# Windowed head-wise convolution and ELU feed-forward: the first super tile's TensorE order from a model, a part of a weight copy on ScalarE, new last turns, one load moved

## The chip, the core and the metric

The kernel runs on one core of a Trainium2 chip. Five engines work from queues of their own and meet only at semaphores: TensorE (PE, with its weight load as PEld), VectorE (DVE), ScalarE (ACT), GpSimd (POOL) and SyncE (SP, which here only issues transfers). The metric is device time in microseconds for one execution; lower is better.

## What is computed

`x` is 8 x 4096 x 192, in 8 heads of 24 channels. Each head has 7 weights over the current and the 6 preceding positions, normalised by a softmax. The result is 32768 tokens of 192 values, and goes through a feed-forward layer of width 2048 with ELU:

```python
w = softmax(weight)                                   # (8 heads, 7 taps)
att[b, s, h] = sum over k of w[h, k] * x_pad[b, s + k, h]
h = att @ w_in                                        # 192 -> 2048
g = np.where(h > 0.0, h, np.exp(np.minimum(h, 0.0)) - 1.0)
out = g @ w_out                                       # 2048 -> 192
```

## The kernel before

**Tiling.** A super tile is 1024 tokens; there are 32 (`NS`). Tokens are split in two groups g of 512. The 2048 hidden features are 16 slices q of 128 (`NQ`). A pair step n = 16 s + q (512 in all, `NP`) makes slice q of super tile s for both groups: units (n, 1) and (n, 0).

**What PE does.** The array is used as two row groups rt of 64 rows, which work side by side. Three kinds of items fill it:

- h (line 835): three matmuls of 512 columns for one unit, rt = group. They need the attention result `att` and `w_in`, which stands twice, in partitions 0 to 63 and again in 64 to 127 (the upper half, for row group 1).
- c (line 808): the convolution of a later super tile as matmuls with a band matrix; four items m to a super tile, each with two matmuls in row group 0 and then two in row group 1, into one bank.
- o (line 858): output matmuls of 192 columns. For a half k = 2 s + half (256 tokens) and a group g they add all 16 slices into one accumulator bank. Both row groups write that bank, in turns that are handed over by the semaphore `s_turn`; a turn is a range of slices in one row group.

**One unit's way.** PE makes H in a PSUM bank, ACT writes E = exp(H) (line 608), POOL clamps E to at most 1 (line 565), DVE writes gT = max(H, E - 1) (line 698). H's bank is free only after DVE. PSUM has 8 banks (`NBANK`), shared by units, convs and accumulators.

**What sets the order.** Before anything is emitted, a planner in Python walks through all pair steps with one clock for each row group. Each item has a fixed cost (line 44: 216 ns for h, 82.5 for o, 102.5 for c), a bank is chosen as the one freed first by fixed holding times (line 48), and the items are sorted by their planned clocks into `pe_order`. ACT's, DVE's and SP's orders follow from the same plan. PE executes `pe_order` strictly; `wait_bank` (line 711) waits for whatever held the bank before.

The lines around the change:

- For n < 24 (`UNTIL`) the clocks are held to at least 1160 ns a pair step (`PACE0`); before the steps n = 1, 2 and 3 `warm` plans one matmul on zeros (line 733).
- Convs of super tile 1 are planned at n = 7, 8, 9, 10 (`EARLY_CONV`). The first accumulators start at n = 4 for group 0 and n = 8 for group 1 (`EARLY_O`), one slice a step; from half 1 on a turn has two slices (`QB`).
- The tail (lines 215 to 236): after the last h, row group 0 does its turns of group 0's open halves and then those of group 1, row group 1 the other way round.
- `w_in` comes in three column parts (`WCOLS`). Parts 0 and 1 are copied to the upper half by DVE (line 623), part 2 (slices 8 to 15) by one SP transfer (line 897); an h item of row group 1 with q of 8 or more waits for it on `s_wd` (line 829).
- POOL issues the loads of x (line 483) between its clamps, at the units listed in `x_before` (lines 265 to 274). The second load of the last super tile is cut in two, since its last window ends at the end of x; both parts are issued at the same unit (lines 487 to 489).

```python
    for n in range(NP):
        if 0 < n < EARLY_O[0]:
            warm(WARM[1])
        if n < UNTIL:
            clock[:] = [max(c, PACE0 * n) for c in clock]
```

Of the kernel before, what the change touches and what calls it, by code (L numbers as in the profile page):

```python
# [49 lines left out]
EARLY_CONV = (7, 8, 9, 10)  # L50
EARLY_O = (4, 8)
PACE0, UNTIL = 1160.0, 24
X_AT = ((2, 1, 1), (1, 1, 0))
ZERO_AT = 8


def bass_lightweight_conv__then__act_elu_kernel(
# [36 lines left out]
    def take_bank(what):  # L94
        if what not in bank_of:
            b = min(range(NBANK), key=lambda b: freed[b])
            assert freed[b] < float("inf")
            bank_of[what], prior[what] = b, occupant[b]
            occupant[b], freed[b] = what, float("inf")

    def h_items(n, r):
        def issue(j):
            take_bank(("h", n, r))
            plan.append((clock[r], ("h", n, r, j)))
            freed[bank_of["h", n, r]] = clock[r] + MM_H + HELD["h"] if j == 2 else float("inf")

        return [(MM_H, lambda j=j: issue(j), None) for j in range(3)]

    def c_items(m, rt):
        def issue(q):  # L110
            take_bank(("c", m))
            plan.append((clock[rt], ("c", m, rt, q)))
            if q == HU - 1:
                conv_half[m] = rt + 1
                if rt == 1:
                    freed[bank_of["c", m]] = clock[1] + MM_C + HELD["c"]

        gate = (lambda: conv_half.get(m) == 1) if rt else None
        return [(MM_C, lambda q=q: issue(q), gate) for q in range(HU)]

    def o_items(k, g, rt, qs, visit, first, final):


        todo = [(q, kb) for q in qs for kb in range(2)]

        def issue(i):
            q, kb = todo[i]
            take_bank(("a", k, g))
            starts, ends = first and i == 0, final and i == len(todo) - 1
            item = ("o", k, g, rt, q, kb, visit if starts else None, ends)  # L130
            plan.append((clock[rt] - AHEAD, item))
            if ends:
                visits[k, g] = visit + 1

        gate = lambda: visits.get((k, g), 0) == visit
        return [(MM_O, lambda i=i: issue(i), gate) for i in range(len(todo))]
# [21 lines left out]
    def warm(count):  # L158
        what = ("w", len(plan) + 1)
        take_bank(what)  # L160
        freed[bank_of[what]] = max(clock)
        plan.append((max(clock) - AHEAD, what + (count,)))
        clock[:] = [max(clock)] * 2

    def evacuated(items, k, g):
        took, issue, gate = items[-1]

        def last():
            issue()
            freed[bank_of["a", k, g]] = max(clock) + MM_O + HELD["a"]  # L170

        items[-1] = (took, last, gate)
        return items
# [11 lines left out]

    conv_steps = {}
# [13 lines left out]
    for n in range(NP):  # L200
        if 0 < n < EARLY_O[0]:
            warm(WARM[1])
        if n < UNTIL:
            clock[:] = [max(c, PACE0 * n) for c in clock]
        lists = [[], []]
        convs = conv_steps.get(n, [])
        for m in convs:
            lists[0] += c_items(m, 0)
        lists[0] += block_items(n, 0, 0) + block_items(n, 1, 0) + h_items(n, 0)
        lists[1] += h_items(n, 1)  # L210
        for m in convs:
            lists[1] += c_items(m, 1)
        lists[1] += block_items(n, 0, 1) + block_items(n, 1, 1)
        emit(lists)
    tail = [[], []]
    for second in range(2):
        for rt in range(2):
# [3 lines left out]
            if second == 0:  # L221
                for kk, q0, q1, v, first in (
                    (k, QB * b, late, 2 * b, True),
                    (k + 1, 0, late, 0, True),
                    (k, late, NQ, 2 * b, False),
                    (k + 1, late, NQ, 0, False),
                ):
                    if kk < NK and q0 < q1:
                        tail[rt] += o_items(kk, g, rt, range(q0, q1), v, first, not first)
            else:  # L230
                for kk, q0, v in ((k, QB * b, 2 * b), (k + 1, 0, 0)):
                    if kk < NK:
                        tail[rt] += evacuated(
                            o_items(kk, g, rt, range(q0, NQ), v + 1, True, True), kk, g
                        )
# [28 lines left out]

    x_before = {}
    for s in range(2, NS):
        for u, ahead, gr in X_AT:
            before = 0
            for item in act_order:
                before += item[0] == "h"  # L270
                if item == ("c", CU * s + u):
                    break
            if s + ahead < NS:
                x_before.setdefault(before, []).append((s + ahead, gr))
# [6 lines left out]
    with ExitStack() as stack:  # L281
# [69 lines left out]
        s_wd = sema("s_wd")  # L351
        s_band = sema("s_band")
# [115 lines left out]
        def _gpsimd(g: bass.BassGpSimd):  # L468
            W = Waits(g)

            def load_x(s, gr):
# [15 lines left out]
                if s == NS - 1 and gr == 1:  # L487
                    windows(0, NWIN - 1, P)
                    windows(NWIN - 1, NWIN, GS - CW * (NWIN - 1) + PAD)
# [85 lines left out]
        def _scalar(a):  # L575
# [24 lines left out]
            for item in act_order:  # L600
# [4 lines left out]
                elif item[0] == "h":  # L605
# [4 lines left out]
                    ).then_inc(s_exp)  # L610
                else:
# [96 lines left out]
        def _tensor(pe):  # L708
# [16 lines left out]
            for item in pe_order:  # L725
# [94 lines left out]
                elif item[0] == "h":  # L820
                    _, n, r, j = item
                    s, q = divmod(n, NQ)
                    if j == 0:
                        part = next(k for k in range(3) if FC * q < WCOLS[k][1])
                        W(s_w[part], 48)
                        if r == 1 and part < 2:
                            W(s_wc, part + 1)
                        elif r == 1:
# [44 lines left out]
        def _sync(sy):  # L873
# [22 lines left out]
            c0, c1 = WCOLS[2]  # L896
# [42 lines left out]
```

## Time and profile before

| what | value |
|---|---|
| median of four executions | 727.45 us (727.38 to 727.98) |
| the profiled execution, its own time | 727.98 us |
| its span, first to last instruction | 725.9 us |
| granted TensorE clock | 1.00 of full |
| chain that ended last, PE's L858 / L835 / L808 | 53% / 37% / 3% |
| DVE L698, 1024 units | 683 ns mean |
| POOL L565, 1024 units | 612 ns mean |
| ACT L608, 1024 units | 601 ns mean |
| ACT L604, 124 conv copies | 563 ns mean |
| POOL L483, 63 issues of x loads | 901 ns mean |

The span runs from the first to the last instruction that the profiler recorded; the execution's time has some 2 us more around it. Timeline rows give the start, the duration, engine, line, operation and count, and in brackets the idle time just before and what ended it. An instruction's duration has its start-up in it: two ACT or DVE instructions in a row overlap a little, so they start closer together than they last. Matmuls are pipelined: a row of 243 ns stands for one that starts 82.5 ns after the last in its row group. Window rows give, for each engine, busy time and in brackets how many instructions ran.

### The profile page before, as it was taken

To read this page: it belongs to the slowest core of one execution; us is meant where nothing else is said; L and a number is where in the kernel's file an instruction comes from. 1 tells how busy PE (TensorE), PEld (TensorE's weight loads), DVE (VectorE), ACT (ScalarE), POOL (GpSimd) and SP (SyncE) were. 2 spreads that over 40 slices of the span, in tenths; PEclk is the share of its full clock that TensorE was granted. 3 is DMA by queue.
4 is the path that set the end of the run, shared out by engine and by line. 5 is a ranking of instruction groups with operands and counts; after the bars stand their busy time and mean duration, and the time that the engine had idled before them with its cause. 6 is when DMAs were issued, how large, how long until landed. Compare 5 with 4: busy or idle time off the path is not lost.

```text
span 725.9 us, 27612 instructions
## 1 busy us (share of the span) xinstructions
PE 718.2 (99%) x11853; PEld 680.2 (94%) x11854; DVE 641.5 (88%) x1043; ACT 676.8 (93%) x1286; POOL 669.8 (92%) x1115
## 2 busy tenths in 40 slices
PE   9899999999999999999999999999999999999998
PEld 4589999999999999999999999999999999999997
DVE  5898989888989988989988989988989988988993
ACT  5899999999999999999999999999999999999993
POOL 8899999999999999999999999999999999999892
PEclk9999999999999999999999999999999999999999
DMA  9654464553345653545553546652535553645212
GB/s 189 97 85 63 71 89 81 85 97 58 75 82 88 87 83 60 87 75 93 86 90 51 90 73 96 86 86 49 95 73 96 86 68 66 97 72 85 70 34 68
DMA packets 132715, 59.21 MB, mean 82 GB/s; under 512 B 98664, under 2 KB 131824, under 8 KB 132592
## 3 DMA queue, kind: packets, MB, share of 16 engines
q1 hardware_dynamic: 88144, 39.66, 23.9%
q0 software_dynamic: 44032, 16.79, 23.0%
q8 instruction: 93, 1.52, 0.9%
q10 hardware_dynamic: 416, 0.98, 0.4%
q14 instruction: 30, 0.25, 0.1%
HBM read 34.83 MB, written 25.66 MB: 83 GB/s over the span
## 4 chain that ended last, share of the span: by engine, by line
PE 95%; POOL 2%; ACT 1%; DVE 1%; issue 0%; ACTq 0%; DVEq 0%
PE H L858 53%; PE H L835 37%; PE H L808 3%; POOL E L565 1%; DVE gT L698 1%; ACT E L608 1%; PE H L786 1%; ACT csb L604 0%; POOL xg L483 0%; PE H L759 0%; PE H L733 0%; ACT L580 0%; ACT osb L612 0%; DVE osb L689 0%; ACTq L577 0%
## 5 line engine op out<-in xcount | busy, mean ns | idle before, releaser
L698 DVE SCALAR_TENSOR_TENSOR gT<-E,H 128x512 f16<-128x512 f32 x1024 | 633.0, 683 | 67.9 <-POOL E L565 66.5
L858 PE MATMUL H<-w_out,gT 64*128 64x192 f16 x8192 | 684.4, 243 | 0.2
L835 PE MATMUL H<-att,w_in 64*128 64x512 bf16 x3072 | 681.8, 376 | 1.8 <-DVE gT L698 1.4
L858 PEld LDWEIGHTS H<-w_out,gT 64*128 64x128 f16 x8192 | 627.9, 94 | 20.8 <-PE H L858 2.3
L565 POOL TENSOR_SCALAR E<-E 128x512 f32<-128x512 f32 x1024 | 606.6, 612 | 42.8 <-ACT E L608 31.2
L608 ACT ACTIVATE E<-H 128x512 f32<-128x512 f32 x1024 | 593.8, 601 | 30.0 <-PE H L835 4.0
L835 PEld LDWEIGHTS H<-att,w_in 64*128 64x128 bf16 x3072 | 274.5, 93 | 8.8 <-issue 2.1
L808 PE MATMUL H<-xg,Tm 64*112 64x240 bf16 x496 | 92.5, 266 | 0.9 <-ACT csb L604 0.9
L604 ACT ACTIVATE csb<-H 112x480 bf16<-112x480 f32 x124 | 69.9, 563 | 0.0
L612 ACT ACTIVATE osb<-H 128x384 f32<-128x384 f32 x127 | 61.7, 486 | 7.5 <-PE H L858 7.4
L808 PEld LDWEIGHTS H<-xg,Tm 64*112 64x112 bf16 x496 | 57.3, 125 | 4.6 <-ACT csb L604 1.6
L483 POOL DMA_DIRECT2D xg<-in_x_dram x63 | 56.4, 901 | 0.2 <-issue 0.2
L689 DVE COPY osb<-H 128x384 f32<-128x384 f32 x1 | 0.6, 558 | 8.5 <-PE H L858 8.5
L733 PE MATMUL H<-zw 128*128 128x512 bf16 x13 | 5.8, 574 | 1.3 <-DVE zw L625 1.3
L501 POOL DMA_DIRECT2D w_in<-in_moe_w_in_dram x9 | 5.3, 655 | 0.0
L733 PEld LDWEIGHTS H<-zw 128*128 128x128 bf16 x13 | 1.5, 125 | 4.0 <-issue 2.7
L786 PE MATMUL H<-xT,taps 128*128 128x256 bf16 (+1 forms) x27 | 4.5, 323 | 0.2 <-issue 0.2
L786 PEld LDWEIGHTS H<-xT,taps 128*128 128x128 bf16 x28 | 2.6, 97 | 1.9
L599 ACT ACTIVATE att<-H 128x512 bf16<-128x512 f32 (+1 forms) x2 | 1.0, 490 | 3.4 <-PE H L786 3.4
L587 ACT ACTIVATE xb<-xs 128x512 bf16<-128x512 f32 x3 | 1.7, 618 | 2.5 <-DMA xs<-in_x_dram 2.5
L512 POOL DMA_DIRECT2D w_out<-in_moe_w_out_dram x3 | 2.8, 988 | 0.0
L623 DVE COPY w_in<-w_in 64x1536 bf16<-64x1536 bf16 x2 | 2.2, 1080 | 0.6 <-DMA w_in<-in_moe_w_in_dram 0.5
(38 smaller groups left out, 17.0 us busy)
## 6 DMA issues: line engine op xcount, KB each, us to landing
out_dram<-osb SPq DMA_DIRECT2D x127, 192.0 KB, 3.3
xg<-in_x_dram POOLq DMA_DIRECT2D x61, 240.0 KB, 5.0
xs<-in_x_dram ACTq DMA_DIRECT2D x1, 768.0 KB, 4.7
att<-csb SPq DMA_TRANSPOSE x31, 4.6
conv_band<-wband SPq DMA_DIRECT2D x1, 480.0 KB, 5.4
Tm<-conv_band SPq DMA_DIRECT2D x1, 448.0 KB, 6.8
w_in<-in_moe_w_in_dram POOLq DMA_DIRECT2D x6, 64.0 KB, 3.0
w_in<-in_moe_w_in_dram POOLq DMA_DIRECT2D x3, 128.0 KB, 5.6
```

The source lines that it names most:

```text
L483: g.dma_start(xg[0:rows, b, 2 * w0 + gr : 2 * w1 : 2, :], src).then_inc(s_x[b][gr], 16)
L501: g.dma_start(w_in[0:HP, j, c0:c1], bass.AP(tensor=moe_w_in.tensor, offset=8 * j * FF + c0, ap=[[CPH * FF, HEADS], [FF, 8], [1, c1 - c0]], ...
L565: g.tensor_scalar(out=E[:, i % NE, :], in0=E[:, i % NE, :], scalar1=1.0, scalar2=0.0, op0=ALU.min, op1=ALU.max,).then_inc(s_clp)
L604: a.activation(*conv_evac(W, m), ACT.Copy).then_inc(s_ce)
L608: a.activation(E[:, i % NE, :], H[:, bank_of[item], :], ACT.Exp).then_inc(s_exp)
L612: a.activation(*out_evac(W, *item[1:]), ACT.Copy).then_inc(s_oev[item[2]])
L698: v.scalar_tensor_tensor(out=gT[:, s % NG3, q, u, :], in0=E[:, i % NE, :], scalar=1.0, in1=H[:, bank_of[item], :], op0=ALU.subtract, op1=A ...
L733: pe.matmul(H[:, bank, :], zw[:, 0:P], zw[:, 0:GS], start=True, stop=True)
L786: ins = pe.matmul(H[:, bank_of[item] + part, c0:c1], taps[:, tap, :], xT[:, j, HALO - PAD + tap + c0 : HALO - PAD + tap + c1], start=(tap ...
L808: ins = pe.matmul(H[0:CW, bank_of["c", m], 256 * q : 256 * q + UC], Tm[rows, h, 0:CW], xg[rows, s % NXB, :, CPH * h : CPH * (h + 1)].rearr ...
L835: ins = pe.matmul(H[:, bank_of[item[:3]], :], w_in[HP * r : HP * (r + 1), j, FC * q : FC * (q + 1)], att[HP * r : HP * (r + 1), s % 2, j, ...
L858: ins = pe.matmul(acc_of(k, g)[:, D * kb : D * (kb + 1)], gT[HP * rt : HP * (rt + 1), t % NG3, q, g, t0 : t0 + P], w_out[HP * rt : HP * (r ...
```

## The change

- A new function `live` plans the first 16 pair steps (`LIVE`). It holds lists of h, c and o work for each row group and always takes the item that can start first, by a model of ACT, POOL and DVE (`act`, `elu`) with durations and hand-over times as constants, and of the landing of x, `w_in` and `w_out` (`LANDS`). The turns of half 0 in this stretch are the same slices as before (12 of group 0, 8 of group 1), but start when the model has gT ready. Bank times in this stretch come from the model.
- The three `warm` items and the pacing by `PACE0` go.
- ACT copies the upper half of `w_in` for slices 8 and 9 behind the exponential of unit 6 (`COPY_AT`); SP's transfer has slices 10 to 15 (`LATE_Q`). h items of row group 1 wait for `s_wa` at slices 8 and 9 and for `s_wd` from 10 on.
- In the tail, first turns: `lead` slices of the last half (12 in row group 0, 4 in row group 1, so that with the first half's there are `TAIL` = 18) stand ahead of the last two slices of the half before, instead of 14.
- The second part of the last super tile's second x load is issued one conv item later.

```diff
...
 EARLY_CONV = (7, 8, 9, 10)
+LATE_Q, COPY_AT = 10, 6
+LIVE, UNTIL = 16, 16
 EARLY_O = (4, 8)
-PACE0, UNTIL = 1160.0, 24
+LANDS = {"x": {1: 7200.0, 2: 14200.0}, "w_in": 10200.0, "w_out": (3900.0, 8400.0, 11000.0)}
+DONE_PE, TO_ACT, TO_POOL, TO_DVE, TO_PE = 165.0, 40.0, 85.0, 35.0, 60.0
+ACT_H, ACT_C, ACT_O, POOL_H, DVE_H = 495.0, 470.0, 390.0, 578.0, 600.0
+ENDS_ACT, ENDS_POOL, ENDS_DVE, TRANSPOSED = 103.0, 37.0, 84.0, 5000.0
+TURNS = 260.0
 X_AT = ((2, 1, 1), (1, 1, 0))
 ZERO_AT = 8
+TAIL = 18
...
-    def take_bank(what):
+    busy = {"act": 0.0, "pool": 0.0, "dve": 0.0}
+    gt_at, turned, att_at, conv_begun, step = {}, {}, {0: 0.0}, {}, [0]
+    def act(at, took):
+        busy["act"] = max(busy["act"], at + DONE_PE + TO_ACT) + took
+        return busy["act"] + ENDS_ACT
+    def elu(n, r, at):
+        end = act(at, ACT_H)
+        busy["pool"] = max(busy["pool"], end + TO_POOL) + POOL_H
+        busy["dve"] = max(busy["dve"], busy["pool"] + ENDS_POOL + TO_DVE) + DVE_H
+        gt_at[n, r] = freed[bank_of["h", n, r]] = busy["dve"] + ENDS_DVE + TO_PE
+    def modelled():
+        return step[0] < UNTIL
+    def take_bank(what, rt):
         if what not in bank_of:
             assert freed[b] < float("inf")
+            if modelled():
+                clock[rt] = max(clock[rt], freed[b])
             bank_of[what], prior[what] = b, occupant[b]
         def issue(j):
-            take_bank(("h", n, r))
+            take_bank(("h", n, r), r)
             plan.append((clock[r], ("h", n, r, j)))
-            freed[bank_of["h", n, r]] = clock[r] + MM_H + HELD["h"] if j == 2 else float("inf")
+            if j == 2:
+                freed[bank_of["h", n, r]] = clock[r] + MM_H + HELD["h"]
+                if modelled():
+                    elu(n, r, clock[r] + MM_H)
         def issue(q):
-            take_bank(("c", m))
+            take_bank(("c", m), rt)
             plan.append((clock[rt], ("c", m, rt, q)))
                     freed[bank_of["c", m]] = clock[1] + MM_C + HELD["c"]
+                    if modelled():
+                        freed[bank_of["c", m]] = act(clock[1] + MM_C, ACT_C) + TO_PE
...
             q, kb = todo[i]
-            take_bank(("a", k, g))
+            take_bank(("a", k, g), rt)
+            if modelled():
+                t = NQ * (k // 2) + q
+                clock[rt] = max(clock[rt], gt_at[t, g], turned.get((k, g), 0.0) if first and i == 0 else 0.0)
             starts, ends = first and i == 0, final and i == len(todo) - 1
                 visits[k, g] = visit + 1
+                turned[k, g] = clock[rt] + MM_O + TURNS
...
-    def warm(count):
-        what = ("w", len(plan) + 1)
-        take_bank(what)
-        freed[bank_of[what]] = max(clock)
-        plan.append((max(clock) - AHEAD, what + (count,)))
-        clock[:] = [max(clock)] * 2
     def evacuated(items, k, g):
             freed[bank_of["a", k, g]] = max(clock) + MM_O + HELD["a"]
+            if modelled():
+                freed[bank_of["a", k, g]] = act(max(clock) + MM_O, ACT_O) + TO_PE
...
+    def live(last, convs, turns):
+        hq = [list(range(last)) for _ in range(2)]
+        cq = [list(convs), list(convs)]
+        far = float("inf")
+        def h_ready(rt):
+            if not hq[rt]:
+                return far
+            n = hq[rt][0]
+            s, q = divmod(n, NQ)
+            if len(hq[1 - rt]) > len(hq[rt]) + (rt == 0):
+                return far
+            if s not in att_at:
+                return far
+            late = rt == 1 and s == 0 and q >= LATE_Q
+            return max(min(freed), att_at[s], LANDS["w_in"] if late else 0.0)
+        def c_ready(rt):
+            if not cq[rt]:
+                return far
+            at, m = cq[rt][0]
+            if last - len(hq[0]) < at:
+                return far
+            if rt:
+                return conv_begun.get(m, far)
+            return max(min(freed), LANDS["x"].get(m // CU, 0.0))
+        def o_ready(rt, g):
+            if not turns[rt][g]:
+                return far
+            k, q0, q1, visit, *_ = turns[rt][g][0]
+            if visits.get((k, g), 0) != visit:
+                return far
+            t = max(gt_at.get((NQ * (k // 2) + q, g), far) for q in range(q0, q1))
+            if k < 2:
+                t = max(t, LANDS["w_out"][next(i for i in range(3) if q1 <= WOUT[i + 1])])
+            if visit == 0:
+                return max(t, min(freed))
+            return max(t, turned[k, g])
+        while any(hq) or any(cq) or any(map(any, turns)):
+            best = None
+            for rt in range(2):
+                for rank, (what, at) in enumerate(
+                    (
+                        (("c",), c_ready(rt)),
+                        (("h",), h_ready(rt)),
+                        (("o", 0), o_ready(rt, 0)),
+                        (("o", 1), o_ready(rt, 1)),
+                    )
+                ):
+                    if at < far:
+                        opens = rank > 1 and turns[rt][what[1]][0][3] == 0
+                        key = (max(at, clock[rt]), 0 if opens else rank)
+                        if best is None or key + (1 - rt,) < best[0]:
+                            best = (key + (1 - rt,), rt, what)
+            assert best is not None
+            (t, *_), rt, what = best
+            clock[rt] = t
+            def go(items):
+                for took, issue, _ in items:
+                    issue()
+                    clock[rt] += took
+            if what[0] == "h":
+                n = hq[rt].pop(0)
+                go(h_items(n, rt))
+            elif what[0] == "c":
+                _, m = cq[rt].pop(0)
+                go(c_items(m, rt))
+                if rt == 0:
+                    conv_begun[m] = clock[0] + DONE_PE + 100.0
+                else:
+                    if m % CU == CU - 1:
+                        att_at[m // CU] = freed[bank_of["c", m]] + TRANSPOSED
+            else:
+                g = what[1]
+                k, q0, q1, visit = turns[rt][g].pop(0)
+                go(o_items(k, g, rt, range(q0, q1), visit, True, True))
+        clock[:] = [max(clock)] * 2
     conv_steps = {}
...
         bank_of.setdefault(what, b)
-    for n in range(NP):
-        if 0 < n < EARLY_O[0]:
-            warm(WARM[1])
-        if n < UNTIL:
-            clock[:] = [max(c, PACE0 * n) for c in clock]
+    turns = [[[], []], [[], []]]
+    for rt in range(2):
+        for g in range(2):
+            turns[rt][g] += [(0, q, q + 1, 2 * q + rt) for q in range(LIVE - EARLY_O[g])]
+    live(LIVE, [(n, m) for n in range(LIVE) for m in conv_steps.get(n, ())], turns)
+    for n in range(LIVE, NP):
+        step[0] = n
+        if n == UNTIL:
+            clock[:] = [max(clock)] * 2
         lists = [[], []]
...
             if second == 0:
+                lead = TAIL - (late - QB * b)
                 for kk, q0, q1, v, first in (
                     (k, QB * b, late, 2 * b, True),
-                    (k + 1, 0, late, 0, True),
+                    (k + 1, 0, lead, 0, True),
                     (k, late, NQ, 2 * b, False),
-                    (k + 1, late, NQ, 0, False),
+                    (k + 1, lead, NQ, 0, False),
                 ):
-                    if kk < NK and q0 < q1:
-                        tail[rt] += o_items(kk, g, rt, range(q0, q1), v, first, not first)
+                    tail[rt] += o_items(kk, g, rt, range(q0, q1), v, first, not first)
             else:
                 for kk, q0, v in ((k, QB * b, 2 * b), (k + 1, 0, 0)):
-                    if kk < NK:
-                        tail[rt] += evacuated(
-                            o_items(kk, g, rt, range(q0, NQ), v + 1, True, True), kk, g
-                        )
+                    tail[rt] += evacuated(
+                        o_items(kk, g, rt, range(q0, NQ), v + 1, True, True), kk, g
+                    )
     emit(tail)
...
+    def h_before(item):
+        return sum(what[0] == "h" for what in act_order[: act_order.index(item)])
     x_before = {}
         for u, ahead, gr in X_AT:
-            before = 0
-            for item in act_order:
-                before += item[0] == "h"
-                if item == ("c", CU * s + u):
-                    break
             if s + ahead < NS:
-                x_before.setdefault(before, []).append((s + ahead, gr))
+                x_before.setdefault(h_before(("c", CU * s + u)), []).append((s + ahead, gr))
+            if (s + ahead, gr) == (NS - 1, 1):
+                x_before.setdefault(h_before(("c", CU * s + u + 1)), []).append((NS - 1, 2))
...
         s_wd = sema("s_wd")
+        s_wa = sema("s_wa")
         s_band = sema("s_band")
...
                     windows(0, NWIN - 1, P)
+                elif gr == 2:
+                    gr = 1
                     windows(NWIN - 1, NWIN, GS - CW * (NWIN - 1) + PAD)
...
                     ).then_inc(s_exp)
+                    if i == COPY_AT:
+                        c0, c1 = WCOLS[2][0], FC * LATE_Q
+                        W(s_w[2], 48)
+                        a.activation(
+                            w_in[HP:P, :, c0:c1], w_in[0:HP, :, c0:c1], ACT.Copy
+                        ).then_inc(s_wa)
                 else:
...
                             W(s_wc, part + 1)
+                        elif r == 1 and q < LATE_Q:
+                            W(s_wa, 1)
                         elif r == 1:
...
             W(s_w[2], 48)
-            c0, c1 = WCOLS[2]
+            c0, c1 = FC * LATE_Q, FF
             sy.dma_start(w_in[HP:P, :, c0:c1], w_in[0:HP, :, c0:c1]).then_inc(s_wd, 16)
             sync_work = []
...
```

## Prediction

> **What bounds the kernel now.** I read the shares first, then the PE column by stretches, then the elementwise rows and the two ends.
>
> ```profile
> PE 718.2 (99%) x11853; PEld 680.2 (94%) x11854; DVE 641.5 (88%) x1043; ACT 676.8 (93%) x1286; POOL 669.8 (92%) x1115
> ...
> PE   9899999999999999999999999999999999999998
> ...
> PEclk9999999999999999999999999999999999999999
> ...
> PE 95%; POOL 2%; ACT 1%; DVE 1%; issue 0%; ACTq 0%; DVEq 0%
> ```
>
> PE is the bound: 95% of the chain that ended last is PE, and the clock is full in all 40 slices. But the share hides the ends. Windows (engine busy, instruction counts in brackets, then PE clock, DMA share, GB/s):
>
> ```profile
> 15.36:25.02 9.66, 7.83 (x77) 3.86 (x76) 9.66 (x16) 8.42 (x17) 8.92 (x16) 1.00 1.27 209
> 25.02:31.39 6.37, 5.66 (x71) 3.82 (x73) 4.63 (x7) 5.57 (x12) 4.64 (x9) 1.00 0.21 37
> 34.90:45.43 10.53, 10.42 (x138) 7.63 (x137) 9.59 (x17) 9.67 (x20) 10.50 (x18) 1.00 0.30 44
> 45.43:56.46 11.03, 11.03 (x186) 10.51 (x186) 10.13 (x17) 10.73 (x21) 10.15 (x17) 1.00 0.70 100
> ```
>
> Up to 25.02 DVE is busy without a gap: it sets the pace. From 25.02 to 31.39 DVE has only 4.63 of 6.37 us. From 34.90 POOL is full (10.50 of 10.53, a load's issue among its work). From 45.43 the pace is PE's: 11.03 us for eight pair steps, and one super tile takes 21.87 us from then on (first upper H matmul of pairs 32 and 48, found by counting L835 in program order: 56.46 and 78.34). So time saved before about 45 us is kept to the end, unless a later engine eats it.
>
> The hole after 25 us, on ACT:
>
> ```profile
> 24.57 0.56 ACT L604 ACTIVATE csb<-H 112x480 bf16<-112x480 f32 x1
> 25.02 0.60 ACT L608 ACTIVATE E<-H 128x512 f32<-128x512 f32 x1
> 26.00 0.60 ACT L608 ACTIVATE E<-H 128x512 f32<-128x512 f32 x1 [0.38 <-PE H L835]
> 26.49 0.56 ACT L604 ACTIVATE csb<-H 112x480 bf16<-112x480 f32 x1
> ```
>
> Each conv copy starts 1.92 us after the last. Conv items 5, 6 and 7 take the same PSUM bank in turn, so PE waits at each for the copy of the one before, with the H matmuls of the next unit behind it. Just ahead, at 22.31, PE stops until 23.24. The page blames DVE, but the transfer below was issued at 14.45 and landed 8.7 us later, 23.15; the next matmul is the first that needs it.
>
> ```profile
> w_in<-w_in SPq DMA_DIRECT2D x1, 384.0 KB, 8.7
> ```
>
> At the end, L858's windows (PE, PEld):
>
> ```profile
> 716.10:717.25 1.15, 1.15 (x18) 0.97 (x12) 1.00 0.00 0
> 718.00:719.15 1.15, 1.15 (x34) 1.15 (x30) 1.00 0.00 0
> ```
>
> Half as many matmuls start at 716.1: the lower row group stands still, because group 1's first accumulator is closed by the upper row group only after 60 of its matmuls, while the lower one is free after 48.
>
> **Part 1, order of the first super tile.** DVE starts unit 0 at 15.36, unit 15 at 24.34, unit 22 at 30.80, unit 32 at 37.08: 0.60 us a unit, then 0.92, then 0.63. The new order opens both accumulators as soon as gT stands, chooses banks by when the engines are modelled to free them, and puts convs at a modelled landing. What it can win is the 0.92. Floor: 32 units at 0.60 from 15.36 is 34.56, 2.5 us earlier. ACT: exponentials start 0.49 apart when fed, a conv copy takes 0.455. Eight units with four convs cost ACT 8 x 0.49 + 4 x 0.455 = 5.74 us, 0.72 a unit; a lead won earlier at 0.11 a unit covers some. A unit holds its bank 2.85 us from H to gT plus some 0.1; with eight banks less two accumulators and one conv, five give 0.59 a unit with nothing to spare, and each conv copy in ACT's queue adds to the hold. I take 0.67 for the eight conv units, 0.62 for the ten behind: 15.36 + 14 x 0.60 + 8 x 0.67 + 10 x 0.62 = 35.3. A further 0.2 goes because modelled times miss: x is set at 20.14 (12.94 + 7.2) and landed at 20.41, and PE waits in order, all H matmuls behind it. Gain 37.08 - 35.5 = **1.6 us**; ends 2.5 (floor) and 0.6 (conv units at 0.80, the rest at 0.63).
>
> Three warm-up matmuls go, 0.33 us each. PE isn't the limit there and DVE is dense, so 0; but H of pairs 1 to 3 comes some 0.6 us earlier, which lets ACT run dense.
>
> The Trainium skill speaks against this part ("TensorE: Matmul & The Clock Gate", "A second HAM failure mode: psum-queue depth-cycling"): short PE pauses between matmul groups while PSUM banks cycle can throw the array's clock back and forth between half and full. The row: from 15.36 to 25.02 PE was busy 7.83 of 9.66 us and the clock was 1.00. By the rule the super tile's some 14.7 us of PE work (96 H at 216 ns, 80 output at 82.5, 20 conv at 102.5, the spacings of line 44, two row groups side by side) would take 29, ending near 42 instead of 34.9: plus 7. By the row, 0. I take the row, the same bank cycling on this kernel.
>
> **Part 2, copy by ACT.** One Copy of 64x768. The att copies took 383 ns for 256 columns and 597 for 512; so 811, or 0.71 spaced. It stands behind the exponential of unit 6; unit 7's is next in the queue, then POOL and DVE. Fed densely, unit 7 is at 14.03 + 7 x 0.49 + 0.71 = 18.17, and with the 1.33 us that unit 0 took from ACT to DVE at 19.50; DVE is ready for it at 19.56. Hidden, 0.06 to spare; uncovered, 0.7. It spends the lead, which is why I don't take 0.60 for conv units. PE's new wait (pair 8, past 21 us) is over by about 18.4. SP's transfer shrinks from 384 to 288 KB; landing again near 23.15 it is needed at pair 10, unit 20, about 24.5: the 0.93 us stop goes, its gain counted above.
>
> **Part 3, no pacing from pair 16 to 24.** PE was already 3.4 us behind the paced clock (34.90 against 12.94 + 18.56), so pacing delayed nothing. POOL is full in this stretch whatever the order: **0**, ends plus and minus 0.3.
>
> **Part 4, last turns.** The first accumulators now close after 20 slices, 40 matmuls, in each row group: 3.3 us at 82.5 ns. The lower group changes over after 48 (3.96 us) and waits no more; its hole was 1.23 us between starts, less one step 1.15. gT of the last pair ended at 714.38, needed at 712.17 + 36 x 0.0825 = 715.1. Both groups now end together near 721.57; the stores of the last two accumulators, 1.15 us apart before, meet: 0 to 0.3 lost. Gain **1.0**, ends 0.7 and 1.2.
>
> **Part 5, last x piece.**
>
> ```profile
> 658.73 1.36 POOL L483 DMA_DIRECT2D xg<-in_x_dram  x2
> ```
>
> Two issues, 0.79 and 0.57 us, in one place; elsewhere a single 0.90 costs nothing. From pair 474 on PE was 22.30 behind the tile before instead of 21.87: 0.43 lost. Now the second stands four units later; POOL wins back about 0.1 a unit (0.58 against PE's 0.68), so its worst lag is 0.79 - 0.4 + 0.57 = 0.96, near the harmless 0.90. Gain **0.4**, ends 0 and 0.45. New wait: conv 124, at 644.46 + 21.87 = 666.33 by the tile before; the piece is issued at about 640.11 + 21.87 = 661.98. By the row (4.0 us for 26.2 KB, behind the big piece) it lands at 665.98, 0.35 in time; by the skill's "DMA: Bandwidth & Descriptors", "Anatomy of one DMA", some 2 us fixed plus bytes/436 GB/s, 2.1, at 664.1. Either way 0. I keep the row: a landing 0.8 us later would eat the gain.
>
> **Sum.** 1.6 + 0 + 1.0 + 0.4 = 3.0 us. The profiled execution took 727.98 (span 725.85 and 2.13 around it): 725.0. The median shown is 727.45, 0.5 lower, so **724.5**.
>
> **Rivals.** (B) *ACT becomes the bound of the first tile*: copy and convs undo the order's gain, leaving parts 4 and 5: 727.45 - 1.4 = 726.05. For it: no lead is left at unit 7. Against: 0.92 a unit is far above ACT's 0.72. (C) *Elementwise floor*: 2.5 + 0.3 + 1.2 + 0.4 = 4.4, 723.05. For it: the dense stretch before; against: five banks with no slack. (D) *Slower: bank starvation*. Both accumulators are open from about 16 us instead of 17 and 23.5, so H has six banks, not seven, and five with a conv, while the modelled order leaves out ACT's copy; one late bank holds the whole in-order PE queue. Before, units 0 to 32 averaged 0.68 us. At 0.72 they eat parts 4 and 5; at 0.77 the sum is +1.5: 728.95. That needs a hold of 5 x 0.77 = 3.85 us against 2.95. Against it: in units 24 to 36 both accumulators were open and the rate was 0.62.
>
> **Chances.** Forecast 0.58 (723.4 to 725.6), B 0.22, C 0.12, D 0.08. The range 722.9 to 726.3 leaves out D and the edges of B and C. A measurement tells about 0.2%, 1.45 us: faster means below 726.0. Forecast, C and half of B are faster: 0.82; the other half of B, 0.11, same; 0.07 slower.
>
> **What would show it.** Right: DVE starts unit 32 near 35.5; conv copies less than 1.7 us apart; no PE stop of 0.9 near 22.3; 34 output matmuls, not 18, in each 1.15 us window of the tail, which lasts 9.4 us from the last H matmul, not 10.5; pairs 474 to 490 at 21.87 behind the tile before. Wrong: gaps on DVE behind the copy at unit 7, PE waits at an accumulator's first matmul or at conv 4 and 124, a granted clock below 1.00, or stretches after 45 us longer than before.

## The result and the profile after

| | before | changed kernel |
|---|---|---|
| median | 727.52 us (63 runs) | 726.60 us (42 runs) |
| ratio, 95% interval | | 0.9987 [0.9982, 0.9991] |
| profiled execution, its span | 727.98, 725.9 us | 726.20, 724.1 us |
| first H matmul to first of pair 32 | 43.52 us | 42.07 us |
| pair 464 to pair 480 (tile 29) | 22.32 us | 22.96 us |
| last PE matmul to end of span | 3.12 us | 3.63 us |

The change saves 0.9 us, about 0.13%, and the interval reaches from 0.65 to 1.3 us. The forecast was 3.0 us. The last three rows, found by counting PE's matmuls in program order, show where the forecast and the result part: the first super tile won 1.45 us, one place near 665 us lost 0.64 us more than before, and the end gave back part of what the tail won.

The page first (busy time, share of the span, instructions; then PE and its clock in 40 slices).

```profile
PE 717.1 (99%) x11850; PEld 679.5 (94%) x11851; DVE 640.6 (88%) x1043; ACT 677.2 (94%) x1287; POOL 669.5 (92%) x1115
...
PE   8999999999999999999999999999999999999997
...
PEclk9999999999999999999999999999999999999999
```

The clock stays full, so the pauses between bank hand-overs cost no speed. The start, in windows placed as before but 0.32 us earlier, since the first H matmul came at 12.62 instead of 12.94 us (the last two are again pair steps 16 to 24 and 24 to 32):

```profile
15.04:24.70 9.66, 9.36 (x95) 5.27 (x92) 9.52 (x16) 9.45 (x19) 9.19 (x16) 1.00 1.36 211
24.70:31.07 6.37, 6.37 (x72) 4.33 (x68) 5.74 (x10) 6.37 (x14) 5.47 (x11) 1.00 0.42 77
32.72:43.66 10.94, 10.69 (x140) 7.59 (x137) 10.23 (x18) 9.97 (x21) 10.77 (x19) 1.00 0.29 42
43.66:54.69 11.03, 11.03 (x186) 10.54 (x186) 10.14 (x17) 10.72 (x21) 10.16 (x17) 1.00 0.69 98
```

In the second window DVE works 5.74 of 6.37 us, where it worked 4.63, and ACT is now the full one. In the third, POOL works 10.77 of 10.94 us, and the eight pair steps take 0.4 us more than before. The fourth is the pace of PE, 11.03 as before.

The copies of convs 4 to 7 on ACT, which stood 2.15, 1.92 and 1.92 us apart, are now 2.21, 0.93 and 1.40 us apart:

```profile
22.37 0.57 ACT L723 ACTIVATE csb<-H 112x480 bf16<-112x480 f32 x1
...
24.58 0.56 ACT L723 ACTIVATE csb<-H 112x480 bf16<-112x480 f32 x1
25.03 0.60 ACT L727 ACTIVATE E<-H 128x512 f32<-128x512 f32 x1
25.51 0.58 ACT L723 ACTIVATE csb<-H 112x480 bf16<-112x480 f32 x1
...
26.91 0.61 ACT L723 ACTIVATE csb<-H 112x480 bf16<-112x480 f32 x1
```

At 665 us PE stops, with no engine named (L962 is the line of the H matmuls in the changed kernel, L933 that of the convs, L985 that of the output matmuls):

```profile
664.74 0.38 PE L962 MATMUL H<-att,w_in 64*128 64x512 bf16 x1
665.70 0.28 PE L933 MATMUL H<-xg,Tm 64*112 64x240 bf16 x1 [0.59 <-issue]
```

This is conv 124, the first of the last super tile. It waits for the x piece that was moved. The row of the piece, then that of the transpose, both issued just after 659.7 us (KB, microseconds from issue to landing):

```profile
xg<-in_x_dram POOLq DMA_DIRECT2D x1, 26.2 KB, 5.5
att<-csb SPq DMA_TRANSPOSE x1, 6.0
```

POOL's timeline has the issue at 660.07, so the piece landed at 665.6, and conv 124 followed some 0.1 us later. "Issue" in the brackets thus stands for the landing of a transfer.

In the tail there is no half-empty stretch any more; one window of it (L985 alone, PE and PEld):

```profile
715.00:716.15 1.15, 1.15 (x34) 1.15 (x30) 1.00 0.00 0
```

Last, the store behind the very last accumulator, issued from ACT's queue:

```profile
out_dram<-osb ACTq DMA_DIRECT2D x1, 192.0 KB, 2.5
```

It took 2.0 us before, when it ran alone at the end.

### The profile page after: what moved, and what is told of

Its sections match the earlier page's. It is cut to its first block, busy times and chain, and to the rows that moved or that the text cites. A ratio compares the mean times of both kernels' runs of the same rounds, so it can differ in the third digit from the quotient of the medians.

```text
span 724.1 us, 27607 instructions
## 1 busy us (share of the span) xinstructions
PE 717.1 (99%) x11850; PEld 679.5 (94%) x11851; DVE 640.6 (88%) x1043; ACT 677.2 (94%) x1287; POOL 669.5 (92%) x1115
## 4 chain that ended last, share of the span: by engine, by line
PE 94%; POOL 2%; ACT 1%; DVE 1%; DMA 1%; issue 0%; DVEq 0%
PE H L985 53%; PE H L962 37%; PE H L933 3%; POOL E L684 2%; DVE gT L823 1%; ACT E L727 1%; DMA xs<-in_x_dram 1%; PE H L911 1%; POOL xg L600 0%; ACT csb L723 0%; PE H L884 0%; ACT osb L737 0%; ACT xb L706 0%; DVE osb L814 0%; PE H L895 0%
## 5 line engine op out<-in xcount | busy, mean ns | idle before, releaser
L985 PE MATMUL H<-w_out,gT 64*128 64x192 f16 x8192 | 682.5, 243 | 0.1
L962 PE MATMUL H<-att,w_in 64*128 64x512 bf16 x3072 | 681.1, 376 | 0.4 <-DVE gT L823 0.2
L985 PEld LDWEIGHTS H<-w_out,gT 64*128 64x128 f16 x8192 | 626.2, 94 | 21.6 <-PE H L985 1.4
L962 PEld LDWEIGHTS H<-att,w_in 64*128 64x128 bf16 x3072 | 274.9, 93 | 7.9 <-DVE gT L823 1.0
L933 PE MATMUL H<-xg,Tm 64*112 64x240 bf16 x496 | 92.6, 266 | 0.7 <-issue 0.6
L933 PEld LDWEIGHTS H<-xg,Tm 64*112 64x112 bf16 x496 | 57.2, 125 | 4.2 <-DVE gT L823 1.1
L858 PE MATMUL H<-zw 128*128 128x512 bf16 x10 | 4.0, 561 | 1.2 <-DVE zw L750 1.2
```

What stands on the lines that cost most here:

```text
L858: pe.matmul(H[:, bank, :], zw[:, 0:P], zw[:, 0:GS], start=True, stop=True)
L933: ins = pe.matmul(H[0:CW, bank_of["c", m], 256 * q : 256 * q + UC], Tm[rows, h, 0:CW], xg[rows, s % NXB, :, CPH * h : CPH * (h + 1)].rearr ...
L962: ins = pe.matmul(H[:, bank_of[item[:3]], :], w_in[HP * r : HP * (r + 1), j, FC * q : FC * (q + 1)], att[HP * r : HP * (r + 1), s % 2, j, ...
L985: ins = pe.matmul(acc_of(k, g)[:, D * kb : D * (kb + 1)], gT[HP * rt : HP * (rt + 1), t % NG3, q, g, t0 : t0 + P], w_out[HP * rt : HP * (r ...
```

## The experiments

Ratios are to the kernel before, timed beside each run on the same chip; its median there was 727.3 to 727.9 us. Brackets hold 95% intervals.

**The piece back in its old place** (`e1_both`), and **the piece ahead of everything** (`e2_early`):

```diff
-                x_before.setdefault(h_before(("c", CU * s + u + 1)), []).append((NS - 1, 2))
+                x_before.setdefault(h_before(("c", CU * s + u)), []).append((NS - 1, 2))        # e1_both
+                x_before.setdefault(h_before(("c", CU * s + u)) - 5, []).append((NS - 1, 2))    # e2_early
```

> The changed kernel with the last x piece issued where the kernel before issues it, directly behind the other part. Theory (the moved piece lands behind the transpose of att, so conv 124 waits for it): the 1.09 us lost at pair 478 of the profile go, the 0.43 us of the double issue come back, so 0.66 us less than the changed kernel: about 725.9 us, conv 124 within 0.45 us of one tile period (21.87) behind conv 120. Rival (the stop at 665.7 us has another cause, the transpose itself or POOL's queue): conv 124 is still 1 us late and the time stays at 726.6 us or rises.

> The changed kernel with the last x piece issued five units ahead of the big part (at unit 938 instead of 947), well before the transpose. Theory (only the landing behind the transpose hurts): no stop at conv 124 and no lag from a double issue, 1.1 us less than the changed kernel: about 725.5 us, pairs 478 to 490 within 0.1 us of 21.87 behind the tile before. Rival (each further issue on POOL costs PE time wherever it stands): pairs from 474 on again about 22.3 behind the tile before, about 725.9 us.

`e1_both` took 725.54 us, ratio 0.9976 [0.9967, 0.9985]; `e2_early` 725.55, 0.9972 [0.9963, 0.9982]. In `e1_both` conv 124 began 22.25 us behind conv 120, 0.38 over a tile period and so at the lag of the double issue alone; tile 29 took 22.32 us as in the kernel before. The stop thus comes with the move and goes with it. In `e2_early` conv 124 didn't wait for the piece, whose row there is

```profile
xg<-in_x_dram POOLq DMA_DIRECT2D x1, 26.2 KB, 2.7
```

Its time is the theory's, but its trace is the rival's: the pairs from 474 on are 22.30 us behind the tile before, as late as with the double issue, and pairs 472 and 473 already 0.2 us. Five units are too few for POOL to make up for an issue before the next one.

The time from issue to landing leaves out how the piece got late. This is what the core's DMA engines moved in the changed kernel from 662 to 666 us, in slices of 0.1 us, and one packet of the queue that brings instructions:

```profile
GB/s 218 207 200 218 215 224 230 220 251 222 407 125 59 146 230 23 0 0 0 0 6 10 9 6 10 10 10 13 128 238 200 376 376 246 16 0 0 0 0 0
...
q8 instruction: 1, 0.02, 1.6%
```

From 662.0 on the packets of the piece go out between those of the transpose. At 663.03 the instruction packet (16 KB) starts, and 0.3 us later 20 packets of the other queues stand still, for 1.3 to 1.5 us each. Of the 16 completion signals of the piece six had come by 663.3, the other ten came from 664.9 to 665.6. All four profiles with the piece in this place have such a stop, of 1.2 to 1.7 us (`after`, `e4_piece`, `e5_nocopy`, `e7_nostore`; landings after 5.4 to 5.9 us). It is not special to the piece: in the 14 traces of this case each of the 152 transposes that had more than 100 of its 1680 packets to go when an instruction packet started has 17 or more packets that stand for over 0.9 us, and only 20 of the other 282 have 15 or more. In the kernels with the piece in its old place the instruction packet came when the packets of this transpose were all but out (at 3.50 us behind its issue, with the last packet at 3.48, in the kernel before). An estimate from the first six signals: without the stop the piece would have landed near 664 us, before conv 124 was due at 665.1. So what made it late is a transfer in flight together with the transpose and an instruction packet; no run takes one of the two away and leaves the other.

**The tail alone** (`e3_tail`) and **the moved piece alone** (`e4_piece`), on the kernel before:

```diff
+                lead = TAIL - (late - QB * b)                                     # e3_tail
-                    (k + 1, 0, late, 0, True),
+                    (k + 1, 0, lead, 0, True),
...
-                    (k + 1, late, NQ, 0, False),
+                    (k + 1, lead, NQ, 0, False),
+            if (s + ahead, gr) == (NS - 1, 1):                                    # e4_piece
+                x_before.setdefault(h_before(("c", CU * s + u + 1)), []).append((NS - 1, 2))
```

> The kernel before with the new last turns alone. Theory (PE's hole goes, but the last two stores now run side by side): PE's last matmul ends 1.15 us earlier counted from the first H matmul, from there to the end of the span takes 3.65 instead of 3.12 us, net 0.6 us: about 726.9 us. Rival (stores side by side cost nothing and the profile's end is chance): 1.15 us less, 726.35 us. Second rival (the end is set by the stores alone): no gain, 727.5 us.

> The kernel before with the moved x piece alone. Theory (it lands behind the transpose): conv 124 waits about 1.1 us, the 0.43 us of the double issue are won, so 0.66 us more: about 728.2 us. Rival (the move works as forecast and the stop in the changed kernel comes from its other order): 0.4 us less, 727.1 us.

`e3_tail`: 726.56 us, 0.9991 [0.9982, 1.0]; PE ended 10.05 us behind the first matmul of its last H unit instead of 11.20, and the stretch behind it grew from 3.12 to 3.5 us. `e4_piece`: 727.95, 1.0008 [0.9998, 1.0017]; the piece landed after 5.9 us and tile 29 took 23.34. By the ratios that is 0.65 us less and 0.58 more than the kernel before, where the theory said 0.6 less and 0.66 more. Both intervals just touch no change; the traces carry the verdict.

**One store less** (`e7_nostore`): the changed kernel without the store of group 0's last 256 rows.

```diff
-                elif item[1:] != (NK - 1, 1):
+                elif item[1] != NK - 1:
...
-                sy.wait_ge(s_out[b], 32 * NS)
+                sy.wait_ge(s_out[b], 32 * NS - 16 * b)
```

> The changed kernel without the store of group 0's last accumulator (256 rows of the output are left out). Theory (the last two stores run side by side and lengthen each other): from PE's last matmul to the end of the span 3.1 to 3.2 instead of 3.65 us, 0.5 us less: about 726.1 us. Rival (the longer end has another cause, such as ACT's evacuation ahead of the last store): 3.6 us again, 726.6 us.

725.89 us, 0.9978 [0.9969, 0.9987]; last matmul to end 3.3 us. The last store, now alone:

```profile
out_dram<-osb ACTq DMA_DIRECT2D x1, 192.0 KB, 2.1
```

The end is 0.35 us nearer than in the changed kernel. The other profiles say how far this one number can be trusted: in the eight with both stores side by side the last store took 2.3 to 2.9 us and the end came 3.47 to 4.12 us behind the last matmul, in the five with the old last turns 2.0 us and 3.12 to 3.14. The meeting of the stores thus costs 0.35 to 1.0 us, 0.5 in the profile of the changed kernel. With one store gone, 0.15 us of that 0.5 is left over, and its cause is open.

**ACT's copy undone** (`e5_nocopy`):

```diff
-LATE_Q, COPY_AT = 10, 6
+LATE_Q, COPY_AT = 8, -1
```

> The changed kernel without ACT's copy: SP's transfer brings slices 8 to 15 again, as in the kernel before, and the planner takes its landing for all of them. Theory (the copy costs DVE 0.2 us at unit 7 and saves PE's wait of up to 0.9 us for the transfer at pair 8): DVE runs without the gap at unit 7, h of pair 8 in row group 1 waits until the transfer lands at about 23, unit 32 on DVE starts 0.2 to 0.6 us later counted from the first H matmul: 726.6 + 0.4 = 727.0 us. Rival (ACT is the bound of the first tile, so the copy costs its 0.7 us): 726.0 us.

726.56 us, 0.9986 [0.9977, 0.9994]: the same as with the copy, within an interval of 0.6 us to either side. Both expectations missed. SP's whole transfer landed at 21.68 us in this run, not 23.15, ahead of the first H matmul that needs it (23.57), so there was no stop to save; and the first H to pair 32 took 41.97 us, 0.1 less than with the copy. Neither a gain nor a loss from part 2 of the change can be seen here.

**Where the first super tile's gain comes from.** First, other banks for the convs of the kernel before (`e6_convbank`), then another place for them in its order (`e9_convlast`), last the new order alone (`e12_orderonly`).

```diff
-                    freed[bank_of["c", m]] = clock[1] + MM_C + HELD["c"]
+                    freed[bank_of["c", m]] = clock[1] + MM_C + HELD["c"] + (2000.0 if m < 2 * CU else 0.0)
```

> The kernel before with one number changed in its planner: the four convs of super tile 1 are planned to hold their bank 2 us longer, so that convs 5, 6 and 7 get three different banks; order by fixed costs, pacing and warm-up matmuls stay. Theory (the gain of the first super tile is mainly the end of the chain conv - copy - next conv through one bank): copies 5 to 7 less than 1.7 us apart, unit 32 on DVE at about 36.0 instead of 37.1 us, 1 us less: 726.5 us. Rival (the gain needs the new order, with both accumulators opened at once): unit 32 within 0.3 us of 37.1, 727.5 us.

727.86 us, 1.0003 [0.9995, 1.0011]: no gain, and copies still 1.9, 2.0 and 1.8 us apart, though the banks differ. The theory of one bank fell. PE's timeline of this run shows other waits:

```profile
23.87 0.39 PE L835 MATMUL H<-att,w_in 64*128 64x512 bf16 x1
...
24.36 0.39 PE L835 MATMUL H<-att,w_in 64*128 64x512 bf16 x1
...
24.96 0.39 PE L835 MATMUL H<-att,w_in 64*128 64x512 bf16 x1 [0.21 <-DVE gT L698]
```

In program order the first two are the second and third H matmul of unit (8, 1), whose first stood at 23.26. Conv 5, waiting for a bank until DVE freed it at 23.71, was between the first and the second; the first matmul of group 1's accumulator, waiting for a bank until 24.30, was between the second and the third. At 24.96 unit (8, 0) starts, again a wait for DVE, and conv 5's upper half stood behind it. So a unit that is begun is held up by other items that wait for banks. That it then holds its own bank for longer, so that DVE frees the next one later, is a reading of this order, and the next run tests the part of the convs.

```diff
-        for m in convs:
+        early = n < NQ
+        for m in convs * (not early):
             lists[0] += c_items(m, 0)
...
+        for m in convs * early:
+            for rt in range(2):
+                lists[rt] += c_items(m, rt)
```

> The kernel before, where the planner puts the early convs of a step (pair steps 7 to 14) behind the H and output items of that step instead of in front of H of row group 0 and between the two H units. Theory (in the kernel before each conv waits for the next free bank with the H matmuls of a unit already begun behind it in PE's queue, and unit 16 to 22 come 0.92 us apart for that, whichever bank it is): a conv then waits behind finished H, the units 16 to 22 come 0.75 us apart or less, unit 32 on DVE at 36.2 us or earlier, 0.8 us less: 726.6 us. Rival (only the modelled times help, not the place of the convs): unit 32 within 0.3 us of 37.1, 727.4 us.

727.44 us, where the kernel before had 727.90; the ratio over all executions is 0.9987 [0.9976, 0.9997], that of the two medians 0.9994. Units 16 to 22 came 0.78 us apart (0.90 in the kernel before, counted the same way), and unit 32 started on DVE 23.64 us behind the first H matmul instead of 24.14. By the trace the place of the convs is worth a third of the order's 1.44 us; it didn't reach the 0.75 expected. The other two thirds are not traced to one item. One candidate is group 1's accumulator: the old order opens it in the middle of pair 8, 10.3 to 11.4 us behind the first H matmul, the new one at 5.56. No run changes that alone.

```diff
-                lead = TAIL - (late - QB * b)
+                lead = late
...
-                x_before.setdefault(h_before(("c", CU * s + u + 1)), []).append((NS - 1, 2))
+                x_before.setdefault(h_before(("c", CU * s + u)), []).append((NS - 1, 2))
```

> The changed kernel with the old last turns and the last x piece in its old place: what stays is the first super tile's order, the copy by ACT and no pacing or warm-up. Theory (the order gives what the profile shows from the first H matmul to that of pair 32, 42.07 instead of 43.52 us): 1.45 us less than the kernel before, a ratio of 0.9980, and in the profile a first tile (pair 0 to pair 16) of 20.1 us, tile 30 of 22.3, the tail with its hole. Rival (the whole change, its tail and its piece as timed one by one leave 0.9 us for the order): 0.9 us less, a ratio of 0.9988.

726.56 us, 0.9988 [0.9979, 0.9996]: 0.9 us, the rival's number, with the theory's 1.45 just inside the interval. The profile has the theory's stretch, 42.07 us, and its first tile of 20.1 us.

**How far away the piece has to stand, and what a single issue costs** (`e8_far`, `e10_far2`, `e11_loads`), all on the changed kernel:

```diff
+                x_before.setdefault(h_before(("c", CU * s + u)) - 20, []).append((NS - 1, 2))       # e8_far, e11_loads
+                x_before.setdefault(h_before(("c", CU * s + u)) - 24, []).append((NS - 1, 2))       # e10_far2
+                x_before.setdefault(h_before(("c", CU * s + u)) - 3, []).append((s + ahead, gr))    # e11_loads
```

> The changed kernel with the last x piece issued at unit 923, 20 units ahead of the big part and 10 ahead of the load before it, so far from every other issue. Theory (an issue costs PE something only where POOL hasn't made up for the one before): pairs 474 to 477 within 0.05 us of 21.87 behind the tile before, where five units of distance left 0.2 and the double issue 0.43; 0.2 us less than with five units, 1.1 less than the changed kernel: about 725.4 us. Rival (each further issue costs 0.2 us wherever it stands): 22.1, 725.6 us.

> The changed kernel with the last x piece at unit 919, four units further ahead than in the run that took 724.4 us. That run was 0.9 us better than its theory, because every tile, long before the piece, took 21.84 instead of 21.87 us, its x issues 0.888 instead of 0.901 us. Theory A (that was chance of one load of the program or its placement): tiles of 21.87 again, about 725.3 us. Theory B (it comes with the moved piece): 21.84 and 724.4 us.

> The changed kernel with the last x piece at unit 923 and all x loads from super tile 3 on issued three units earlier (the last piece 20 units ahead of its old place as before). Theory (a single issue of 0.90 us is not free: in every tile the conv two units behind the first load waits 0.03 us for a bank that DVE frees late because POOL was held up): with three units more to recover, tiles take 21.84 us or less, 0.9 us less than 725.3: about 724.4 us. Rival (POOL's lag only meets another item): 21.87, 725.3 us or more.

`e8_far`: 724.43 us, 0.9953 [0.9941, 0.9965], the fastest of all; `e10_far2`: 725.37, 0.9959 [0.9944, 0.9973], where the kernel before had 727.90. In `e8_far` pairs 474 to 477 were 21.82 us behind the tile before, no longer late. In `e10_far2` 0.2 us were lost earlier, at pair 463, just behind the piece's new place, and not won back: 22.05 at these pairs. So the theory holds for one of the two places. `e8_far` is 0.9 us better than expected: a tile took 21.84 instead of 21.87 us, long before the piece is issued. Laid beside the changed kernel, the 0.03 us come at one conv in each tile, behind the first x load, whose issue took 0.888 us on POOL instead of 0.901. `e10_far2` has 0.890 and 21.85. Why the issue is shorter in these two programs is open, and that it is the cause of the shorter tile was not tested.

`e11_loads`, which differs from `e8_far` only in the three units, settles that the place of an issue is not free, with the opposite sign to the one expected: 740.83 us, 1.0166 [1.0145, 1.0186], tiles of 22.42 us. PE, which has no wait of this kind between 300 and 330 us in the changed kernel, now waits in every tile (of the view of this stretch, three lines):

```profile
PEld H L985 <- DVE gT L823: 0.5, 1, 0.5
PEld H L962 <- DVE gT L823: 0.3, 2, 0.2
PE H L985 <- DVE gT L823: 0.2, 1, 0.2
```

The first is the first matmul of a new accumulator, which has to have the bank of a unit that DVE finishes late. Three units earlier, as we read it, POOL's lag of 0.9 us meets the opening of the accumulator instead of falling between two.

## Why the prediction was wrong, point by point

- **What bounds it**: right. PE's pace of 11.03 us for eight pair steps is unchanged behind 45 us, and what was won in front of it stayed won.
- **Part 1**, forecast 1.6 us: the slow stretch shrank, but not for the reason given, so that the profile's number comes near is partly luck. In the profile 1.45 us (unit 32 on DVE 22.70 us behind the first H matmul instead of 24.14); timed alone 0.9 [0.3, 1.5]. The reason given for the hole, three convs through one bank, fell with `e6_convbank`; a third of the gain on DVE belongs to the convs' place in PE's queue (`e9_convlast`), the rest is not taken apart. Conv units came 0.71 us apart, not 0.67: that is ACT's own 0.72, which the prediction had worked out, and ACT is full there now (6.37 of 6.37 us). The ten behind came at 0.60, not 0.62. "A unit holds its bank 2.85 us" was the shortest hold: in the kernel before the units of pairs 8 to 11 held theirs 2.85 to 3.69 us, from the first H matmul to the end of gT. The stop at 22.3 us was not a gain of 0.93 us either: in `e6_convbank` the transfer landed 7.51 us behind the first H matmul instead of 10.21, PE didn't stop there, and unit 32 came 0.1 us sooner. The granted clock stayed 1.00; the row was the right choice against the rule.
- **Part 2**: forecast hidden. Not quite: the copy held ACT for 0.86 us and not 0.71, and DVE started unit 7 at 6.83 instead of 6.61 us behind the first H matmul, as the text had named for a sign of being wrong. By unit 32 nothing of it can be seen (`e5_nocopy`, 0.1 us).
- **Part 3**: forecast 0, ends plus and minus 0.3; the stretch of pairs 16 to 24 took 10.94 instead of 10.53 us in the profile. That is no loss: PE reached pair 16 earlier by 1.85 us, DVE its unit 32 by 1.43, and from unit 32 to unit 64 DVE took 21.78 us, before 21.81.
- **Part 4**, forecast 1.0: PE's hole went as worked out, 1.15 us. Mis-sized was "the stores of the last two accumulators meet: 0 to 0.3 lost", taken as 0.15. It is 0.5 in this profile (3.63 against 3.12 us) and 0.35 to 1.0 in all, which leaves 0.64; timed alone, 0.65.
- **Part 5**, forecast a gain of 0.4: **this step failed**. It is the landing, "By the row (4.0 us for 26.2 KB, behind the big piece) it lands at 665.98, 0.35 in time", and "I keep the row". That row had been measured with the piece right behind the big part and ahead of the transpose. Moved, it is issued 0.28 us behind the transpose of the tile before; it landed after 5.4 to 5.9 us in the four profiles of that kind, conv 124 waited, and tile 29 took 22.96 us where 21.9 was forecast and 22.32 had been. The text named the point from which it tips, "a landing 0.8 us later would eat the gain", and conv 124 among the signs of being wrong, but that the move passes SP's transpose was not considered. The Trainium skill says in "DMA: Bandwidth & Descriptors", "Issuing engines are not separate DMA queues", that transfers of all issuing engines run on the same 16 DMA engines and interleave; the packets from 662.0 us on agree. Had SP's row at 661.56 been read beside POOL's 661.98, the row of 4.0 would have had no standing. Sharing with the transpose is still only half of it; the stop behind the instruction packet is the other. The estimate from the page's section "Anatomy of one DMA", 2.1 us, is near what the piece takes with no other packet in flight, 2.0 us in `e8_far`. "Its worst lag is near the harmless 0.90" was wrong too, by 0.2 us: pairs 476 to 478 were that late before the stop.

Under "Chances", 0.58, 0.12 and 0.11 add up to 0.81, not 0.82.

By single runs: the order 0.87 less, the tail 0.65 less, the piece 0.58 more, together 0.94 less; measured 0.95 on the same ratio. Each of the three was timed with an interval of about 0.6 us to either side. Against 1.6, 1.0 and 0.4 less, the forecast missed 0.7 at the order, 0.4 at the tail and 1.0 at the piece.

What stays open is why the order gives more in the profiles than when timed. From the first H matmul to pair 32 the four profiles with the old order took 43.39 to 44.21 us (`before`, `e3_tail`, `e4_piece`, `e6_convbank`), the nine with the new one 41.97 to 42.39. So the profile of the kernel before was not alone in its first tile. But the four executions with the old order lay 0.5 to 1.4 us above their medians, those with the new within 0.4 of theirs, and `e9_convlast`, old order with the convs moved, 0.3 below. Part of this lies ahead of the first H matmul, which came at 12.45 to 14.02 us, whatever the order. Whether the profiled executions of the old order were slow ones in the first tile too, no run shows.

The version that beats both kernels is the changed one with the piece at unit 923 or 919: 724.4 and 725.4 us.

## What to carry to other kernels

A step that is moved takes its transfer past other queues: list what each of them issues in the new place, and read a landing time only from a row with the same transfers in flight. Give a load that an engine will wait for a place with no transpose near it. Removing a wait at the end of a kernel can bring two stores together, so follow the sum to the last landing and not to the last matmul. In an in-order queue, put an item that waits for a buffer behind the work that is already begun, not between its parts: here that was worth 0.5 us on DVE.

## What the runs showed of the hardware that was not expected

One 26.2 KB load took 2.0 us from issue to landing with no other packet in flight, 2.2 to 2.9 in three other early places, 3.9 to 4.2 behind a 192 KB load, and 5.4 to 5.9 behind a DMA transpose issued some 0.3 us before it. An instruction packet of 16 KB that starts while a transpose has more than 100 packets to go went with a stop of 17 or more DMA packets for over 0.9 us, in 152 of 152 cases; the transpose's packets then took 3.07 us from first to last, otherwise 2.16 (medians). Of two 192 KB stores side by side the later one took 2.3 to 2.9 us instead of 2.0 to 2.1. The time that POOL needs for issuing the same load differed between programs, 0.901 against 0.888 us, and the tile with it, 21.87 against 21.84 us, which is 0.8 us over the run.
